# A GpSimd drain behind the last scatter of every span of 512 rows in the products stage

## The chip, the cores and the metric

The kernel runs on one core of one Trainium2 chip. The metric is the device time of one execution in microseconds (us); the median of three runs stands for the kernel.

## The reference

The program is a chain of three layers over 8 batches of 3072 tokens of 256 numbers:

```python
x = np.fft.fft(np.fft.fft(x, axis=1), axis=2).real       # transform
logits = x[:3072] @ w_gate                               # routing: one of 8 experts a token,
idx = argmax(logits); gate = softmax(logits)[idx]        # the first 768 tokens of each are kept
h = relu(disp @ w1[e]);  y = h @ w2[e]                   # experts, 256 -> 1024 -> 256
x = gate * y  (kept tokens; all other rows are 0)
a = x @ mw1;  b = x @ mw2                                # gated product layer
out = ((a * b) @ w3) @ w_out
```

(The routing runs over all 24576 tokens; since a row that is not kept gives zeros, the last layer is needed for the 8 x 768 = 6144 kept rows alone.)

## The kernel before, in words

The kernel has three stages. The transform stage computes the Fourier transforms of three batches (of the third, half the rows) on TensorE, routes their tokens, and scatters the kept rows into a table in DRAM (`disp`) with 61 indirect DMAs that GpSimd issues (L509). The experts' stage reads that table expert by expert and leaves its result transposed in SBUF (`yt`, 256 x 6144); meanwhile SyncE writes zeros over the whole output.

The third stage is `products` (L854 and after). It takes the 6144 rows in 12 spans of 512 (`spans`). For a span, `ysplit` makes a high part (ScalarE cast, L159) and a low part (a GpSimd subtraction, L160, tile `yl`) of each half of `yt`, two GpSimd instructions a span. `product` then runs eight times: the two matrix products with three TensorE passes each (L163 to L165), ScalarE copies one out of PSUM, VectorE multiplies by the other (L884), and the product is split again (L159 ScalarE, L160 VectorE). `project` multiplies the eight products of the span before by the fused matrix `Wc` (L896 to L898), 128 rows at a time; ScalarE scales each result by its gate (L900, tile `o`), and GpSimd scatters the 128 rows to their tokens' rows of the output with an indirect DMA (L901). So a span has four scatters, the stage 48. `project` of a span is called after the second `product` of the next one; that of the last span is called at the end. `ysplit` of span n+1 is written down after all of span n's products, but its tiles come from a pool of two buffers (`p_yc`), so it runs as soon as the products of span n-1 have let go of theirs.

The order on the engines in this stage is the scheduler's: the part of the program whose order is given by hand ends ahead of `mlp.products(main)` (L1063). Each engine takes its instructions in order. On GpSimd the stage's queue is: four scatters, two `yl`, four scatters, two `yl`, and so on. The scatters don't wait for one another (`declare_no_dep`); a scatter waits for its `o`.

Behind the stage every engine loads a flag (L1068) and branches (L1069) past a block that repeats the whole work over all batches; with these inputs the block is skipped. On the way past it GpSimd waits for the semaphores of its DMAs and raises them (INC_SWDGE_SEM, L1069). Then the program ends with drains and a barrier of all engines (L1151). GpSimd has a drain among these; the program's beginning has one too (L1144).

Of the kernel before, what the change touches and what calls it, by code (L numbers as in the profile page):

```python
# [125 lines left out]
def body(tc, cap, x, w_gate, w1, w2, mw1, mw2, w3t, w_out, cF, cS, cM, cR, cG, cI, cH, cT, out):  # L126
    nc = tc.nc
# [27 lines left out]
    def pool(name, bufs, stack, **k):  # L155
        return stack.enter_context(tc.tile_pool(name=name, bufs=bufs, reuse_waits="tile", **k))

    def split(hi, lo, src, eng=nc.vector):
        nc.scalar.copy(hi, src)  # L159
        eng.tensor_sub(lo, src, hi.bitcast(F32))  # L160

    def three(ps, wh, wl, ah, al, first, last):
        nc.tensor.matmul(ps, wh, ah, start=first, stop=False)  # L163
        nc.tensor.matmul(ps, wh, al, start=False, stop=False)  # L164
        nc.tensor.matmul(ps, wl, ah, start=False, stop=last)  # L165
# [384 lines left out]
    class Mlp:  # L550
# [303 lines left out]
        def products(self, stack):  # L854

            p_yc = pool("p_yc", 2, stack)
            p_g = pool("p_g", 10, stack)
            p_t = pool("p_t", 2, stack)
            pa = pool("pa", 2, stack, space=PSUM)
            pb = pool("pb", 2, stack, space=PSUM)  # L860
            po = pool("po", 3, stack, space=PSUM)
            yt, WM, Wc = self.yt, self.WM, self.Wc
            scat = []

            def ysplit(r0, n):
                ys = []
                for m in range(2):
                    hi = p_yc.tile([128, 512], F32R, name=f"yh{m}")[:, :n]
                    lo = p_yc.tile([128, 512], F32R, name=f"yl{m}")[:, :n]
                    split(hi, lo, yt[:, m, r0 : r0 + n], nc.gpsimd)  # L870
                    ys.append((hi, lo))
                return ys

            def product(ys, n, f):
                fs = slice(f * 128, f * 128 + 128)
                a = pa.tile([128, 512], F32, name="ps_a")[:, :n]
                b = pb.tile([128, 512], F32, name="ps_b")[:, :n]
                for w, ps in ((0, a), (1, b)):
                    for k in range(2):
                        three(ps, WM[w][0][:, k, fs], WM[w][1][:, k, fs], *ys[k], k == 0, k == 1)  # L880
                sa = p_t.tile([128, 512], F32, name="sa")[:, :n]
                nc.scalar.copy(sa, a)  # L882
                g = p_t.tile([128, 512], F32, name="g")[:, :n]
                nc.vector.tensor_mul(g, b, sa)  # L884
                hi = p_g.tile([128, 512], F32R, name="gh")[:, :n]
                lo = p_g.tile([128, 512], F32R, name="gl")[:, :n]
                split(hi, lo, g)
                return hi, lo

            def project(r0, n, gs):  # L890
                for t in range(n // 128):
                    col = r0 // 128 + t
                    ps = po.tile([128, 256], F32, name="ps_o")
                    ts = slice(t * 128, t * 128 + 128)
                    for f, (hi, lo) in enumerate(gs):
                        nc.tensor.matmul(ps, hi[:, ts], Wc[0][:, f], start=f == 0, stop=False)  # L896
                        nc.tensor.matmul(ps, hi[:, ts], Wc[1][:, f], start=False, stop=False)  # L897
                        nc.tensor.matmul(ps, lo[:, ts], Wc[0][:, f], start=False, stop=f == 7)  # L898
                    o = p_t.tile([128, 256], F32, name="o", bufs=3)
                    nc.scalar.activation(o, ps, AF.Copy, scale=gate2[:, col : col + 1])  # L900
                    i = nc.gpsimd.indirect_dma_start(  # L901
                        out=out[:, :],
                        out_offset=bass.IndirectOffsetOnAxis(ap=toki[:, col : col + 1], axis=0),
                        in_=o,
                        in_offset=None,
                        bounds_check=TOK - 1,
                        oob_is_err=False,
                    )
                    for q in scat:
                        tc.declare_no_dep(i.ins, q.ins, reason="every token has a row of its own")  # L910
                    scat.append(i)

            done = None
            spans = [(r, min(512, ROWS - r)) for r in range(0, ROWS, 512)]
            ys = ysplit(*spans[0])
            for n, (r0, w) in enumerate(spans):
                gs = []
                for f in range(8):
                    gs.append(product(ys, w, f))
                    if f == 1 and done:  # L920
                        project(*done)
                if n + 1 < len(spans):
                    ys = ysplit(*spans[n + 1])
                done = (r0, w, gs)
            project(*done)


# [227 lines left out]
```

## Time and profile before

| | us |
|---|---|
| median of three runs | 837.95 (837.57 to 837.99) |
| the profiled execution, its own time | 836.56 |
| its span, first to last instruction | 834.8 |
| TensorE busy in the span | 802.4 (96%) |
| GpSimd busy in the span | 149.6 (18%) |
| from the end of the last scatter's record to the end of the span | 14.7 |

The profile is of one execution. A busy time is that of the engine's data path; a drain, a branch, a semaphore instruction or a register load counts as none of it and appears only under its source line, on the engine's sequencer (POOLq is GpSimd's, SPq SyncE's). Of an indirect DMA the profile has two things: a record on GpSimd's own row, and the time from issue until its data has landed.

### The profile page before, as it was taken

The page shows a single profiled execution, that of the slowest core. Times are in us where ns is not written, and L with a number is a line of the kernel's source. Part 1 is how long each engine was busy: PE and PEld are TensorE (multiplying, and loading weights), DVE is VectorE, ACT ScalarE, POOL GpSimd, SP SyncE. Part 2 cuts the span into 40 slices and gives each one's busy share as a digit, 9 for nine tenths or more (in the row PEclk, how much of TensorE's full clock was granted, in tenths as well). Part 3 has the DMA queues.
Part 4 walks back from the last instruction along what each step waited for, and adds up shares of the span by engine and source line. Part 5 has one row for each costly group of instructions (what it writes and reads, how often), then busy time and mean ns, then how long its engine had stood idle before and what let it go on. Part 6 is the DMA issues. An engine that isn't in the chain of part 4 may idle for free.

```text
span 834.8 us, 12890 instructions
## 1 busy us (share of the span) xinstructions
PE 802.4 (96%) x5032; PEld 738.0 (88%) x5032; DVE 453.9 (54%) x874; ACT 370.0 (44%) x756; POOL 149.6 (18%) x139
## 2 busy tenths in 40 slices
PE   9999899799999999999999999999999999999992
PEld 8788799699999999999979899898898998988981
DVE  5676675498878787898542523424225234242230
ACT  2555665265545454565443433424334234243230
POOL 0047588000000000000023112121131122111101
PEclk9999899799999999999999999999999999999996
DMA  9945698476849474877100000000000000000000
GB/s 237 259 132 182 200 316 273 125 220 239 260 147 279 147 245 149 259 219 259 66 1 20 7 27 13 13 26 2 25 20 6 26 14 14 26 7 20 25 10 22
DMA packets 68822, 94.65 MB, mean 113 GB/s; under 512 B 5036, under 2 KB 56280, under 8 KB 67696
## 3 DMA queue, kind: packets, MB, share of 16 engines
q1 hardware_dynamic: 63552, 80.90, 32.0%
q0 software_dynamic: 5200, 12.84, 4.3%
q8 instruction: 41, 0.67, 0.3%
q14 instruction: 29, 0.24, 0.1%
HBM read 55.72 MB, written 39.63 MB: 114 GB/s over the span
## 4 chain that ended last, share of the span: by engine, by line
PE 80%; issue 9%; DVE 4%; DMA 3%; POOL 2%; ACT 1%; POOLq 0%; ACTq 0%; DVEq 0%; SPq 0%
PE ps_h L164 5%; PE ps_h L163 5%; PE ps_y L164 5%; PE ps_h L165 5%; PE ps_y L165 5%; PE ps_y L163 5%; PE ps_a L164 4%; PE ps_b L165 4%; PE ps_a L165 4%; PE ps_b L164 4%; PE ps_b L163 4%; PE ps_a L163 4%; PE ps_o L898 4%; PE ps_o L897 4%; PE ps_o L896 4%
## 5 line engine op out<-in xcount | busy, mean ns | idle before, releaser
L884 DVE TENSOR_TENSOR g<-ps_b,sa 128x512 f32<-128x512 f32 x96 | 66.2, 690 | 185.8 <-PE ps_b L165 179.2
L159 ACT CAST gh<-g 128x512 fp32r<-128x512 f32 x96 | 59.6, 620 | 132.9 <-DVE g L884 131.8
L160 DVE TENSOR_TENSOR gl<-g,gh 128x512 fp32r<-128x512 f32 x96 | 76.8, 800 | 65.9 <-ACT gh L159 65.9
L807 ACT ACTIVATE hh<-ps_h 128x256 fp32r<-128x256 f32 (+1 forms) x160 | 67.8, 427 | 97.3 <-PE ps_h L165 92.3
L897 PE MATMUL ps_o<-wcl,gh 128*128 128x256 f32 x384 | 108.7, 283 | 0.0
L898 PE MATMUL ps_o<-wch,gl 128*128 128x256 f32 x384 | 108.7, 283 | 0.0
L896 PE MATMUL ps_o<-wch,gh 128*128 128x256 f32 x384 | 108.6, 283 | 0.0
L160 POOL TENSOR_TENSOR yl<-yt,yh 128x512 fp32r<-128x512 f32 x24 | 30.5, 1288 | 419.5 <-ACT yh L159 419.5
L808 DVE SCALAR_TENSOR_TENSOR hl<-ps_h,hh 128x256 fp32r<-128x256 f32 (+1 forms) x160 | 74.8, 472 | 33.7 <-ACT hh L807 33.3
L509 POOL DMA_INDIRECT disp<-O,sloti x61 | 71.4, 1171 | 75.2 <-DVE acc L523 49.1
L901 POOL DMA_INDIRECT out_dram<-o,toki x48 | 47.0, 979 | 175.2 <-ACT o L900 175.2
L163 PE MATMUL ps_a<-yh,wm0h 128*128 128x512 f32 x192 | 75.0, 390 | 1.0 <-ACT yh L159 1.0
L164 PE MATMUL ps_a<-yl,wm0h 128*128 128x512 f32 x192 | 75.0, 391 | 0.7 <-POOL yl L160 0.7
L164 PE MATMUL ps_b<-yl,wm1h 128*128 128x512 f32 x192 | 74.7, 389 | 0.0
L165 PE MATMUL ps_a<-yh,wm0l 128*128 128x512 f32 x192 | 74.7, 389 | 0.0
L163 PE MATMUL ps_b<-yh,wm1h 128*128 128x512 f32 x192 | 74.7, 389 | 0.0
L165 PE MATMUL ps_b<-yh,wm1l 128*128 128x512 f32 x192 | 74.7, 389 | 0.0
L896 PEld LDWEIGHTS ps_o<-wch,gh 128*128 128x128 f32 x384 | 73.7, 192 | 0.5
L897 PEld LDWEIGHTS ps_o<-wcl,gh 128*128 128x128 f32 x384 | 73.7, 192 | 0.5
L898 PEld LDWEIGHTS ps_o<-wch,gl 128*128 128x128 f32 x384 | 73.7, 192 | 0.0
L900 ACT ACTIVATE o<-ps_o,gate 128x256 f32<-128x256 f32 x48 | 22.8, 475 | 104.7 <-PE ps_o L898 104.7
L882 ACT COPY sa<-ps_a 128x512 f32<-128x512 f32 x96 | 56.3, 587 | 11.6 <-PE ps_a L165 11.4
(179 smaller groups left out, 1952.9 us busy)
## 6 DMA issues: line engine op xcount, KB each, us to landing
out_dram<-zer SPq DMA_DIRECT2D x48, 512.0 KB, 6.5
raw<-in_w_dram SPq DMA_DIRECT2D x44, 512.0 KB, 5.2
xr<-in_x_dram SPq DMA_DIRECT2D x11, 768.0 KB, 8.4
raw<-in_w3t_dram SPq DMA_DIRECT2D x16, 512.0 KB, 4.8
raw<-in_mw_dram SPq DMA_DIRECT2D x8, 512.0 KB, 4.3
X<-disp SPq DMA_DIRECT2D x12, 266.0 KB, 4.2
X<-disp SPq DMA_DIRECT2D x8, 399.0 KB, 6.0
raw<-in_w_out_dram SPq DMA_DIRECT2D x4, 512.0 KB, 4.7
```

What stands on the lines that cost most here:

```text
L159: nc.scalar.copy(hi, src)
L160: eng.tensor_sub(lo, src, hi.bitcast(F32))
L163: nc.tensor.matmul(ps, wh, ah, start=first, stop=False)
L164: nc.tensor.matmul(ps, wh, al, start=False, stop=False)
L165: nc.tensor.matmul(ps, wl, ah, start=False, stop=last)
L509: i = nc.gpsimd.indirect_dma_start(out=disp[:, :], out_offset=bass.IndirectOffsetOnAxis(ap=sloti[0:w, g : g + 1], axis=0), in_=o[0:w, j, c ...
L807: nc.scalar.activation(hi, ps, AF.Relu)
L808: nc.vector.scalar_tensor_tensor(lo, ps, 0.0, hi.bitcast(F32), ALU.max, ALU.subtract)
L884: nc.vector.tensor_mul(g, b, sa)
L896: nc.tensor.matmul(ps, hi[:, ts], Wc[0][:, f], start=f == 0, stop=False)
L897: nc.tensor.matmul(ps, hi[:, ts], Wc[1][:, f], start=False, stop=False)
L898: nc.tensor.matmul(ps, lo[:, ts], Wc[0][:, f], start=False, stop=f == 7)
```

## The change

`project` issues one drain on GpSimd behind the last of its scatters. `i` is that scatter; `tc.issue_after(i.ins)` orders the drain behind it in GpSimd's queue and adds no wait of its own. Nothing else is changed.

```diff
                     for q in scat:
                         tc.declare_no_dep(i.ins, q.ins, reason="every token has a row of its own")
                     scat.append(i)
+                with tc.issue_after(i.ins):
+                    nc.gpsimd.drain()
 
             done = None
             spans = [(r, min(512, ROWS - r)) for r in range(0, ROWS, 512)]
```

There are 12 such drains in the executed path. `products` is called a second time inside the block that is skipped.

## Rows read from the trace of the kernel before

**Rows 1.** The page's busy times, and its 40 slices of the span.
```profile
PE 802.4 (96%) x5032; PEld 738.0 (88%) x5032; DVE 453.9 (54%) x874; ACT 370.0 (44%) x756; POOL 149.6 (18%) x139
PE   9999899799999999999999999999999999999992
POOL 0047588000000000000023112121131122111101
```

**Rows 2.** Busy time of each engine in stretches of the products stage and behind it.
```profile
core 0: us, PE busy (x) PEld busy (x) DVE busy (x) ACT busy (x) POOL busy (x), PEclk, DMA share, GB/s
480.00:520.00 40.00, 40.00 (x250) 36.24 (x249) 12.70 (x17) 14.22 (x25) 8.42 (x8) 1.00 0.05 18
640.00:680.00 40.00, 40.00 (x228) 35.27 (x227) 16.41 (x21) 16.05 (x29) 9.01 (x8) 1.00 0.04 14
825.00:834.00 9.00, 0.00 (x0) 0.00 (x0) 0.00 (x0) 0.00 (x0) 0.00 (x0) 0.50 0.00 0
```

**Rows 3.** GpSimd's timeline in the products stage: start, duration, instruction, idle before and releaser.
```profile
458.25 0.97 POOL L901 DMA_INDIRECT out_dram<-o,toki  x1 [1.95 <-ACT o L900]
473.88 2.54 POOL L160 TENSOR_TENSOR yl<-yt,yh 128x512 fp32r<-128x512 f32 x2 [14.65 <-ACT yh L159]
...
507.18 2.54 POOL L160 TENSOR_TENSOR yl<-yt,yh 128x512 fp32r<-128x512 f32 x2 [14.65 <-ACT yh L159]
...
782.56 0.97 POOL L901 DMA_INDIRECT out_dram<-o,toki  x1 [23.64 <-ACT o L900]
...
810.42 0.97 POOL L901 DMA_INDIRECT out_dram<-o,toki  x1 [18.20 <-ACT o L900]
...
819.10 0.97 POOL L901 DMA_INDIRECT out_dram<-o,toki  x1 [1.95 <-ACT o L900]
```

**Rows 4.** Waits in the products stage: who for whom, us in total, times, longest.
```profile
PEld ps_a L164 <- POOL yl L160: 1.6, 2, 0.8
PE ps_a L164 <- POOL yl L160: 0.7, 2, 0.4
```

**Rows 5.** The last pieces of the chain that ended last: start, duration, what.
```profile
817.15 1.72 issue
818.87 0.49 POOLq L1068
819.36 0.71 POOL out_dram L901
```

**Rows 6.** GpSimd's sequencer by line behind the stage: durations in ns (min/median/max), first and last start.
```profile
L1068 POOLq TENSOR_LOAD <-flagi x1: 492/492/492, 818.9 to 818.9; - x1
L1069 POOLq COMPARE_BRANCH  x1: 53/53/53, 819.4 to 819.4; - x1
L1069 POOLq EVENT_SEMAPHORE  x5: 17/43/43, 822.1 to 822.5; - x5
L1069 POOLq INC_SWDGE_SEM  x1: 2368/2368/2368, 822.6 to 822.6; - x1
L1151 POOLq DRAIN  x3: 40/107/8967, 825.0 to 834.5; - x3
```

**Rows 7.** The last line of Rows 6 cut to 824 to 834 us.
```profile
L1151 POOLq DRAIN  x1: 8967/8967/8967, 825.0 to 825.0; - x1
L1151 POOLq EVENT_SEMAPHORE  x1: 17/17/17, 834.0 to 834.0; - x1
```

**Rows 8.** The stage's scatters by line, and their way from issue to landing.
```profile
L901 POOL DMA_INDIRECT out_dram<-o,toki x48: 972/975/997, 449.6 to 819.1; - x48
DMA to landing us min/median/max: 2.4/2.4/2.5
```

**Rows 9.** DMA traffic from 822.8 us to 834.7 us.
```profile
DMA packets 0, 0.00 MB, mean 0 GB/s; under 512 B 0, under 2 KB 0, under 8 KB 0
```

**Rows 10.** The program's beginning on GpSimd's sequencer (L1144), and the transform stage's scatters.
```profile
L1144 POOLq INC_SWDGE_SEM  x1: 27/27/27, 0.1 to 0.1; - x1
L1144 POOLq DRAIN  x1: 189/189/189, 0.3 to 0.3; - x1
...
L509 POOL DMA_INDIRECT disp<-O,sloti x61: 914/977/2018, 50.4 to 147.0; - x61
```

## The prediction

> **What bounds the kernel now.** I read the page's 40 slices first: TensorE is at nine tenths or more in nearly every slice but the first and the last, GpSimd at one or two tenths in the products stage, and the last slice is almost empty for both [rows 1]. Then the stage's stretches: in the middle of it TensorE is busy 40.00 of 40 us, GpSimd some 8 to 9 [rows 2]. So within the stage nothing that GpSimd does costs time as long as TensorE finds its operands. That leaves the end. By the chain's last pieces, GpSimd's register load (818.87) and the last scatter (819.10, 0.97 us, so over at 820.07) come last [rows 3, 5], and after them no engine's data path does anything. The rest of the span, 834.8 - 820.07 = 14.7 us, is to be read on GpSimd's sequencer, by source line [rows 6, 7]: register load from 818.87, branch at 819.4, first instruction behind the branch at 822.1, INC_SWDGE_SEM 2.37 us from 822.6, and then one drain from 825.0 that lasts **8.967 us**, to 834.0. The final barrier is 0.8 us behind it. So this drain is the bound of the end of the program: whatever shortens it or moves it shows one for one.
>
> What does it wait for? Not for data: the last scatter lands 2.4 us after issue, at 821.5 [rows 8], and from 822.8 us on no DMA packet moves [rows 9]. Not for a matmul or a vector instruction: from 825 to 834 every engine is at zero [rows 2]. And a drain on GpSimd isn't long in itself: the other two of the program's end take 40 and 107 ns [rows 6], the one at the beginning 189 ns [rows 10]. The long one differs in what GpSimd did since the drain before it: 61 + 48 = 109 scatters [rows 8, 10], and the INC_SWDGE_SEM straight ahead of it. The trace doesn't tell which of these it pays for. That is the whole question of this change.
>
> **The change, part by part.** It adds 12 drains; it removes and moves nothing.
>
> *Eleven drains inside the stage.* Behind each stands, on GpSimd's queue, the two low parts `yl` or the next scatter. After the fourth scatter of a span (458.25 + 0.97 = 459.22) GpSimd has nothing to do until 473.88, 14.65 us [rows 3]; ten spans look like this, and the two gaps without `yl` are 23.64 and 18.20 us [rows 3]. The dearest drain that the trace shows is 8.97 us; it fits into the shortest of these gaps with 5.7 us to spare. If the cover were gone: `yl` is written one period ahead of its use, since it fills the second of two buffers. The period is 507.18 - 473.88 = 33.30 us, the two instructions take 2.54, so TensorE would feel a drain only if it held GpSimd up for some 14.65 + 30 = 45 us. TensorE waited for `yl` only at the start of the stage, 0.7 us in all (1.6 us on its weight loads) [rows 4], ahead of the first drain. Nothing else is queued behind a drain; ScalarE waits for scatters' landings to reuse `o`, and the drains stand behind the scatters. Cost of these eleven: **0**, by either price.
>
> *The twelfth drain, behind the last scatter.* Three things happen. First, GpSimd's sequencer now can't run ahead: before, it loaded the flag at 818.87, while the last scatter still ran; now it gets there only when the scatter is over, at 820.07. That is **+1.2 us** on everything behind it [rows 3, 5]. Second, the drain's own length d. Third, the long drain at 825.0 may get shorter.
>
> *The price of a drain.* Bounds by rows: from below 0.04 us, from above 8.97 us [rows 6]. Between them I read the long drain as work that GpSimd put off and that the drain makes it do: the drain behind it costs 107 ns with nothing left to do, so 8.967 - 0.107 = 8.86 us belongs to the backlog, and spread over 109 scatters that is an estimate of 81 ns for each. I take this reading because something other than a fixed wait must have been left over: GpSimd idled for 14 to 24 us at a time between scatters, all data had landed, and yet 9 us remained at the end. Then the first drain of the stage pays for 61 + 4 scatters, 65 x 81 ns = 5.3 us, and the other ten for 4 each, 0.33 us: all inside the gaps. The twelfth pays 0.33 + 0.107 = 0.4 us on the path. The long drain at the end falls to the nearest row with nothing outstanding, 0.107 us.
>
> Sum: +1.2 (the sequencer held) + 0.4 (twelfth drain) - 8.86 (the long drain) = **-7.3 us**. Against the profiled execution's own 836.56 us (span 834.8, so 1.8 us lie around it) that is 829.3; the median of the runs, 837.95, is 1.4 us above the profiled one, and the forecast is made on it: 837.95 - 7.3 = **830.7 us**.
>
> Its own range: INC_SWDGE_SEM, 2.37 us at the end but 0.03 at the beginning [rows 6, 10], might shrink with the backlog (-2.3, 828.3); of the scatter part, only some may be cleared early (to 831.5 if about 0.8 us stays). So 828.2 to 831.5 for this case.
>
> **The rivals.**
>
> *1. A drain only waits for GpSimd's own instructions, and the long one pays for INC_SWDGE_SEM.* Then the eleven drains and the twelfth cost 0.04 to 0.19 us each, the long one stays at 8.97, and only the held sequencer is left: +1.2 + 0.1 = +1.3, 839.3 us. For it: the long drain follows INC_SWDGE_SEM without a gap, and all scatters were long over. Against it: the program's beginning has an INC_SWDGE_SEM too, and the drain behind it took 0.19 us [rows 10], though that one may have had nothing to raise. The Trainium skill says in "PSUM — Partial Sum Buffer", section "Engine vs sequencer instructions", that a drain waits for the engine to go fully idle. By that rule alone nothing could be put off to a drain from scatters whose records ended long before, and the sum would be this rival's; the trace neither contradicts nor confirms it, since what GpSimd does in these 9 us has no record.
>
> *2. A fixed charge once a scatter has been issued.* The first drain behind any scatter costs 8.97 us, however many there were, and the next one without scatters in between 0.1. The eleven are hidden all the same. The twelfth costs 8.97 on the path, the last falls to 0.107: +1.2 + 8.97 - 8.86 = +1.3, 839.3 us, the same as rival 1 by another way. If the drain also waits for the landing (821.5 instead of 820.07) it is 1.4 more, 840.7. For it: short drains follow the long one at once. Against it: nothing in the trace, since no drain stands behind a few scatters alone.
>
> *3. The charge is paid twice: slower.* As rival 2, but INC_SWDGE_SEM behind the twelfth drain brings the charge back, so that the long drain stays: +1.2 + 8.97 = +10.2, 848.1 us. The place is the twelfth drain alone. It decides from the point where twelfth drain and rest together exceed what the long one gives back; with the long one at 0.107 that is at d = 8.86 - 1.2 = 7.7 us. For it: a scatter and an INC_SWDGE_SEM both stand ahead of the long drain, and each may carry its part. Against it: it needs two causes of about the same size where one explains the row.
>
> *4. The order.* The scheduler gives this stage's order; 12 more instructions could shift it. It would have to put a scatter or `yl` over 30 us later to be felt, so I give it little, and nearly all of that to small losses.
>
> **How the numbers follow.** The backlog read off the trace (830.7): 0.50. Rival 1 (839.3): 0.18. Rival 2: 0.15, of it 0.11 at 839.3 and 0.04 with the landing, 840.7. Rival 3 (848.1): 0.14. Order and the like, slower: 0.03. About 0.2%, 1.7 us, is what a measurement of this kernel can tell from no change; so 836.3 to 839.6 counts as the same. Faster: 0.50. Same: 0.18 + 0.11 = 0.29. Slower: 0.04 + 0.14 + 0.03 = 0.21. The range reaches from the first case's lower end over rivals 1 and 2, 828.2 to 841.0, and leaves out rival 3 and most of the order, under 0.2 together. The likeliest case's own range is 828.2 to 831.5.
>
> **What would show it.** In the changed kernel, GpSimd's drains by line: eleven in the gaps behind the fourth scatters, the first of them longest (5 us by the backlog; all alike, 9 us, by rivals 2 and 3; all near 0.1 by rival 1), the twelfth from 820.1 us, and the length of the drain behind INC_SWDGE_SEM: 0.1 us by the backlog and rival 2, 9 us by rivals 1 and 3. The register load should start not before the twelfth drain's end. TensorE should be busy 40 of 40 us in the stage as before, with its last matmul at the same time, and `yl` should start at the same times in the period. What would make the prediction wrong: a twelfth drain of more than 2 us, or a last drain that stays above 1 us; and in the stage, any wait of TensorE for `yl`.

## The result

The changed kernel takes 830.95 us (median of six runs, 827.18 to 833.75) against 837.97 us (837.44 to 839.72) for the kernel before: 7.0 us less, a ratio of 0.9909 with a 95% interval of 0.9887 to 0.9930. The forecast was 830.7, in a range of 828.2 to 841.0. A second measurement (the run e7 below) gave 830.70 against 837.84, ratio 0.9906 (0.9885 to 0.9926). Every ratio here compares, of each kernel, the runs within 1.5% of its own fastest: on the slower chip of e1 and e2 these are six of the seventeen runs of the kernel before, all six of e1 and nine of e2's twelve.

GpSimd's sequencer in the changed kernel, by source line, durations in ns (min/median/max), then first and last start in us. L913 is the new drain; L1070, L1071 and L1153 are the lines that were L1068, L1069 and L1151 [rows 6, 7].

```profile
L913 POOLq DRAIN  x12: 2850/2857/6588, 454.7 to 815.5; - x12
L1070 POOLq TENSOR_LOAD <-flagi x1: 499/499/499, 820.1 to 820.1; - x1
L1071 POOLq INC_SWDGE_SEM  x1: 189/189/189, 823.6 to 823.6; - x1
L1153 POOLq DRAIN  x3: 46/53/107, 823.9 to 825.1; - x3
L1153 SPq DRAIN  x3: 7/7/13, 824.5 to 824.8; - x3
```

The reader is to see three things. The drain of the program's end is now 0.05 us, after 8.97. INC_SWDGE_SEM, which the change doesn't touch, is 0.19 us after 2.37. And the register load starts at 820.1, long after the last scatter:

```profile
454.89 0.97 POOL L901 DMA_INDIRECT out_dram<-o,toki  x1 [1.96 <-ACT o L900]
470.52 2.54 POOL L160 TENSOR_TENSOR yl<-yt,yh 128x512 fp32r<-128x512 f32 x2 [14.66 <-ACT yh L159]
...
815.75 0.97 POOL L901 DMA_INDIRECT out_dram<-o,toki  x1 [1.95 <-ACT o L900]
```

This is GpSimd's timeline (start, duration, instruction, idle before). The idle time ahead of `yl` is 14.66 us, as before [rows 3]: the drain in that gap cost the queue nothing. From the last scatter's end (816.72) to the end of the span (825.4) it is 8.7 us, where it was 14.7: the tail lost **6.0 us**.

The two spans differ by more, 834.8 - 825.4 = 9.4 us. The other 3.35 us lie ahead of all drains: the last scatter starts at 815.75 instead of 819.10, the stage's others are as much earlier, and the difference arises in the transform and experts' stages. There one and the same ScalarE instruction starts at 137.8 us before and at 141.2 in the changed kernel, a later one at 160.9 and 157.4, so the changed kernel is first behind and then ahead. Here the stretch from 150 to 200 us (busy time of each engine, then the granted clock), the changed kernel first, with a stretch of the products stage below it:

```profile
150.00:200.00 50.00, 49.01 (x345) 48.21 (x346) 41.30 (x87) 26.94 (x57) 0.00 (x0) 1.00 0.71 228
480.00:520.00 40.00, 40.00 (x250) 36.24 (x249) 12.02 (x16) 13.60 (x24) 8.91 (x9) 1.00 0.06 21
```

```profile
150.00:200.00 50.00, 47.82 (x324) 46.88 (x325) 38.89 (x82) 24.74 (x53) 0.00 (x0) 0.92 0.69 222
```

From 150 to 200 us the granted clock was 1.00 in the changed kernel's profile and 0.92 on average in the other. No instruction of that stretch is changed, so I count this as the difference between two executions, not as the change's. The profiled execution of the changed kernel is also its fastest (827.18). Within the products stage TensorE is busy 40.00 of 40 us, as before [rows 2].

### The profile page after: what moved, and what is told of

It is laid out like the page before. It is cut to its first block, busy times and chain, and to the rows that moved or that the text cites. A ratio compares the mean times of both kernels' runs of the same rounds, so it can differ in the third digit from the quotient of the medians.

```text
span 825.4 us, 12902 instructions
## 1 busy us (share of the span) xinstructions
PE 803.3 (97%) x5032; PEld 738.3 (89%) x5032; DVE 453.9 (55%) x874; ACT 369.6 (45%) x756; POOL 147.6 (18%) x139
## 4 chain that ended last, share of the span: by engine, by line
PE 79%; issue 9%; DVE 4%; POOL 2%; DMA 2%; ACT 1%; POOLq 1%; DVEq 0%; ACTq 0%; SPq 0%
PE ps_y L164 5%; PE ps_h L164 4%; PE ps_a L164 4%; PE ps_h L165 4%; PE ps_h L163 4%; PE ps_b L165 4%; PE ps_a L165 4%; PE ps_b L164 4%; PE ps_y L165 4%; PE ps_b L163 4%; PE ps_a L163 4%; PE ps_y L163 4%; PE ps_o L898 4%; PE ps_o L897 4%; PE ps_o L896 4%
## 5 line engine op out<-in xcount | busy, mean ns | idle before, releaser
L509 POOL DMA_INDIRECT disp<-O,sloti x61 | 69.4, 1138 | 75.5 <-DVE acc L523 49.6
```

The costliest lines, as they stand in the source:

```text
L509: i = nc.gpsimd.indirect_dma_start(out=disp[:, :], out_offset=bass.IndirectOffsetOnAxis(ap=sloti[0:w, g : g + 1], axis=0), in_=o[0:w, j, c ...
```

## The experiments

The theory after this result: every scatter leaves something behind, which the next drain works off at a fixed price each; besides, a drain lasts at least until the scatters ahead of it have landed. Rivals: a fixed charge that some drain has to pay once; a charge of the last drain alone.

**e1, only the twelfth drain.**

```diff
-                with tc.issue_after(i.ins):
-                    nc.gpsimd.drain()
+                if r0 // 512 == 11:
+                    with tc.issue_after(i.ins):
+                        nc.gpsimd.drain()
```

> Only the drain behind the last span's scatters is kept; the eleven inside the stage are gone. Backlog theory: this one drain has all 109 scatters to work off and does on the path what the drain of the program's end did before: it runs on for 8 to 11 us behind the last scatter's record, INC_SWDGE_SEM and the end's drain are short (0.2 and 0.1 us), and the time is that of the kernel before plus what the held sequencer costs, 0 to +3 us, so 838 to 841. Rival, a fixed charge that a drain ahead of the branch and INC_SWDGE_SEM avoids: the one drain lasts as long as the twelfth did (3.3 us behind the scatter's record) and the time is that of the changed kernel, about 831.

Measured, GpSimd's sequencer by line:

```profile
L914 POOLq DRAIN  x1: 10180/10180/10180, 870.1 to 870.1; - x1
L1072 POOLq INC_SWDGE_SEM  x1: 189/189/189, 883.9 to 883.9; - x1
L1154 POOLq DRAIN  x3: 34/41/107, 884.2 to 885.4; - x3
...
870.38 0.97 POOL L901 DMA_INDIRECT out_dram<-o,toki  x1 [1.95 <-ACT o L900]
```

The one drain runs on for 9.0 us behind the last scatter (which ended at 871.35; the drain at 880.3), and from that scatter to the end of the span it is 14.35 us, against 14.7 in the kernel before. The fixed charge that the last drain would buy off is out: without the eleven drains inside the stage nothing is won. The chip of this run was slower for every kernel, so only comparisons with the kernel before on that chip count (885.78 us there): 886.72 us, ratio 1.0103 (1.0029 to 1.0176). The medians of all runs lie 0.9 us apart and the tails 0.35 us the other way; the ratio's interval lies above 1 because it sets all six runs of e1 against the six fastest of seventeen, so it shows no loss.

**e2 and e8, eleven drains, the twelfth left out** (the condition is `r0 // 512 < 11`). The kernel ran twice, the second time beside the changed kernel.

> The eleven drains inside the stage are kept, the twelfth, behind the last span, is gone. Backlog theory: only four scatters are left over at the end; INC_SWDGE_SEM and the end's drain take 0.2 to 1 us together, and since GpSimd's sequencer may again load the flag and branch while the last scatter runs, the time is 3 to 4.5 us under that of the changed kernel: 826.5 to 828. Rival, a fixed charge for any scatter since the last drain, paid once: the end's drain is again near 9 us, and the time is that of the kernel before, 838. Rival, the twelfth drain is needed to keep INC_SWDGE_SEM short: INC_SWDGE_SEM takes 2.4 us again and the time is about 829.

> Eleven drains, none behind the last span, beside the changed kernel on the same chip. Backlog theory, now with the prices read from the runs: INC_SWDGE_SEM 0.27 us, the end's drain 0.37 us, and 4.4 us from the last scatter's end to the span's end, against 7 to 8.7 in the changed kernel: 2.5 to 4.3 us faster than the changed kernel, 9 to 11 us faster than the kernel before.

Measured in e2, then in e8:

```profile
L1072 POOLq INC_SWDGE_SEM  x1: 268/268/268, 877.9 to 877.9; - x1
L1154 POOLq DRAIN  x3: 46/107/371, 878.2 to 879.4; - x3
```

```profile
L1071 POOLq TENSOR_LOAD <-flagi x1: 500/500/500, 820.2 to 820.2; - x1
L1072 POOLq INC_SWDGE_SEM  x1: 268/268/268, 823.9 to 823.9; - x1
L1154 POOLq DRAIN  x3: 46/107/371, 824.2 to 825.5; - x3
...
820.47 0.97 POOL L901 DMA_INDIRECT out_dram<-o,toki  x1 [1.95 <-ACT o L900]
```

INC_SWDGE_SEM 0.27 and the drain 0.37 us, for four scatters, the same on both chips; the register load is ahead of the last scatter again (820.2 against 820.47), and from that scatter's end (821.44) to the end of the span (825.8) it is 4.4 us. e2's time is unclear on its chip: 875.37 us against 885.78 by the medians of all runs, 0.988, but a ratio of 0.9964 (0.9908 to 1.0021) by the runs that a ratio compares. e8 took **827.45 us** against 837.84, ratio 0.9875 (0.9851 to 0.9900): 3.25 us below the changed kernel on the same chip (e7, 830.70), as expected. Its median is the lowest of this study. "A fixed charge for any scatter since the last drain" is out: four scatters cost 0.4 us, not 9.

**e7, the changed kernel again.**

> The changed kernel once more, beside the next one on the same chip. Backlog theory: twelfth drain ends 0.2 us behind the landing of the last scatter (2.4 to 4.1 us after its issue), INC_SWDGE_SEM 0.19 us, the end's drain 0.05 us; 14.7 us from the last scatter's end to the span's end become 7 to 8.7 us, and the time is 6 to 8 us below that of the kernel before.

```profile
L913 POOLq DRAIN  x12: 2842/2851/6587, 459.0 to 819.8; - x12
L1071 POOLq INC_SWDGE_SEM  x1: 189/189/189, 827.8 to 827.8; - x1
L1153 POOLq DRAIN  x3: 46/53/107, 828.1 to 829.3; - x3
```

The time is 830.70 us, 7.1 below the kernel before; from the last scatter's end (821.03) to the end of the span (829.6) 8.6 us, as in the first profile. The durations agree to some 20 ns, but for the twelfth drain: 4.39 us here, 4.50 there.

**e3, only the first drain** (the condition is `r0 // 512 == 0`).

> Only the drain behind the first span's scatters is kept (65 scatters ahead of it). Backlog theory, 60 to 115 ns a scatter: that drain again runs 5.4 us behind the scatter's record, and the 44 scatters of the other eleven spans are left for the end: INC_SWDGE_SEM and the end's drain together 3 to 6 us instead of 11.3. A fixed charge would leave them at 11.3 us together, or at 2 to 3 us as for four scatters.

```profile
L914 POOLq DRAIN  x1: 6588/6588/6588, 506.2 to 506.2; - x1
L1072 POOLq INC_SWDGE_SEM  x1: 1068/1068/1068, 870.7 to 870.7; - x1
L1154 POOLq DRAIN  x3: 46/107/3647, 871.8 to 876.0; - x3
```

44 scatters were left, and the end pays 1.07 + 3.65 = 4.7 us, in the forecast's span of 3 to 6. (One run: 878.07 us, on e1's chip.)

**e4, drains far behind the landings, at unequal distances.**

```diff
-        eng.tensor_sub(lo, src, hi.bitcast(F32))
+        return eng.tensor_sub(lo, src, hi.bitcast(F32))
...
-                    split(hi, lo, yt[:, m, r0 : r0 + n], nc.gpsimd)
+                    i = split(hi, lo, yt[:, m, r0 : r0 + n], nc.gpsimd)
                     ys.append((hi, lo))
+                if r0 // 512 in (1, 3, 4, 6, 10):
+                    with tc.issue_after(i.ins):
+                        nc.gpsimd.drain()
```

> No drain stands behind scatters. Five drains stand behind the GpSimd subtractions of the spans with the indices 1, 3, 4, 6 and 10, so that all data of the scatters ahead of each has long landed, and 61, 4, 4, 8 and 16 scatters stand between one drain and the next; 16 are left for the end. Backlog theory: behind the subtraction's record the five last 3.7 to 5 us, twice 0.2 to 0.5, 0.4 to 0.9 and 0.8 to 1.9 us, in proportion to the count, and INC_SWDGE_SEM with the end's drain 0.9 to 2 us. If a drain only waits for landings, all five end with the subtraction (under 0.2 us behind it).

The drains of four stretches (the first holds the one behind 61 scatters, the second the two behind 4, then 8, then 16), and the subtractions that they stand behind:

```profile
L874 POOLq DRAIN  x1: 8580/8580/8580, 465.1 to 465.1; - x1
L874 POOLq DRAIN  x2: 2299/2304/2309, 521.0 to 554.3; - x2
L874 POOLq DRAIN  x1: 2629/2629/2629, 620.9 to 620.9; - x1
L874 POOLq DRAIN  x1: 3279/3279/3279, 754.1 to 754.1; - x1
```

```profile
463.63 5.02 POOL L160 TENSOR_TENSOR yl<-yt,yh 128x512 fp32r<-128x512 f32 x4 [295.55 <-ACT yh L159]
520.33 2.54 POOL L160 TENSOR_TENSOR yl<-yt,yh 128x512 fp32r<-128x512 f32 x2 [14.66 <-ACT yh L159]
...
620.23 2.54 POOL L160 TENSOR_TENSOR yl<-yt,yh 128x512 fp32r<-128x512 f32 x2 [14.65 <-ACT yh L159]
...
753.43 2.54 POOL L160 TENSOR_TENSOR yl<-yt,yh 128x512 fp32r<-128x512 f32 x2 [14.65 <-ACT yh L159]
```

A drain's record begins while the subtraction still runs, so what counts is its end less the subtraction's: for 61 scatters 465.1 + 8.58 - 468.65 = 5.0 us; for 4, 521.0 + 2.31 - 522.87 = 0.4; for 8, 620.9 + 2.63 - 622.77 = 0.76 (0.72 by the unrounded start); for 16, 754.1 + 3.28 - 755.97 = 1.4. At the end, for another 16:

```profile
L1072 POOLq INC_SWDGE_SEM  x1: 508/508/508, 869.1 to 869.1; - x1
L1154 POOLq DRAIN  x3: 46/107/1351, 869.7 to 871.6; - x3
```

The price doesn't depend on how long ago the scatters landed: the 61 had ended 300 us before, and nobody had paid for them in between. (One run: 873.63 us, on e1's chip.) With these runs the end's two terms make a table:

| scatters since the drain before | INC_SWDGE_SEM, ns | drain, ns | kernel |
|---|---|---|---|
| 0 | 189 | 41, 53 | e1, changed |
| 4 | 268 | 371 | e2, e8 |
| 16 | 508 | 1351 | e4 |
| 44 | 1068 | 3647 | e3 |
| 109 | 2368 | 8967 | before |

From the first row and the last: (8967 - 41) / 109 = **82 ns** a scatter for the drain, (2368 - 189) / 109 = **20 ns** for INC_SWDGE_SEM. By these two the rows between should be 369, 1353, 3649 and 269, 509, 1069: all are met within 3 ns. The GpSimd subtractions between the drains (none for the four scatters, 18 for the 44) don't count. Nor does the time since the drain before: the first drain of the stage, with 65 scatters, takes 6.588 us when it comes at 454.7 us (changed kernel) and when it comes at 506.2 us (e3).

**e5, fewer rows to a scatter.**

```diff
-                        out_offset=bass.IndirectOffsetOnAxis(ap=toki[:, col : col + 1], axis=0),
-                        in_=o,
+                        out_offset=bass.IndirectOffsetOnAxis(ap=toki[0:16, col : col + 1], axis=0),
+                        in_=o[0:16],
```

> The kernel before, with each of the 48 output scatters cut from 128 rows to the first 16 (the other rows of the output are left out); no drain is added. The end's drain took 41 ns + 82 ns a scatter in the runs so far, and INC_SWDGE_SEM 189 ns + 20 ns a scatter. If the backlog counts scatters, both stay as in the kernel before, 8.97 and 2.37 us. If it counts rows or descriptors, only an eighth of the 48 is left, as from 61 + 6 scatters: 5.5 us and 1.5 us.

```profile
L1069 POOLq INC_SWDGE_SEM  x1: 2368/2368/2368, 823.1 to 823.1; - x1
L1151 POOLq DRAIN  x3: 40/107/8975, 825.5 to 835.1; - x3
```

Unchanged: the backlog counts instructions, not rows. The time, 837.15 us, is the kernel before's.

**e6, 48 plain DMAs more on GpSimd.**

```diff
                     scat.append(i)
+                    nc.gpsimd.dma_start(out=spare[col * 128 : col * 128 + 128], in_=o[:, 0:8])
```

> The kernel before, with 48 plain DMAs added on GpSimd's queue, one of 128 x 8 numbers into a spare DRAM tile behind each output scatter; no drain is added. If the backlog counts every DMA that GpSimd issues, the end's drain takes 157 x 82 ns = 12.9 us and INC_SWDGE_SEM 3.3 us. If it counts indirect DMAs alone, 8.97 and 2.37 us as before.

```profile
L1071 POOLq INC_SWDGE_SEM  x1: 1195/1195/1195, 824.4 to 824.4; - x1
L1153 POOLq DRAIN  x3: 40/107/4157, 825.7 to 830.4; - x3
...
656.11 0.99 POOL L902 DMA_INDIRECT out_dram<-o,toki  x1 [1.32 <-ACT o L901]
658.73 0.58 POOL L913 DMA_DIRECT2D spare<-o  x1 [1.64 <-issue]
```

Neither answer: 4157 ns and 1195 ns are those of (4157 - 41) / 82 = 50 scatters, with 157 DMAs issued. With no drain added and 48 DMAs more the kernel was faster than before in its one run, 832.84 against 837.84 us. In GpSimd's timeline one thing stands out: a single plain DMA, the 115th DMA that GpSimd issues, starts 1.64 us late, with nothing that the profile shows it to wait for. Two more runs went into this.

**e9, 24 plain DMAs more** (`if col % 2:` ahead of the same line), and **e10, 48 scatters more** (128 rows of 8 numbers each, to a spare tile).

> The kernel before with 24 plain DMAs more on GpSimd's queue (behind every second scatter), so 133 DMAs of GpSimd in all; no drain is added. With 48 more (157 in all) the 115th started 1.6 us late and the end's drain took 4.16 us, as from 50. If something cleared the backlog once, at about the 115th, leaving 7 behind, 133 leave 26 here: end's drain 2.2 us, INC_SWDGE_SEM 0.7 us, and again one late start at the 115th. If plain DMAs themselves don't count and 50 was 48 scatters with two more, or if the backlog is held at 50 from some point on, the end's drain is near 4.1 us again.

> The kernel before with 48 more scatters on GpSimd's queue, each of 128 rows of 8 numbers into a spare DRAM tile, 157 indirect DMAs in all; no drain is added. If what cleared the backlog is the number of GpSimd's DMAs, of whatever kind, the 115th starts late again and the end's drain takes 4.2 us as with 48 plain DMAs. If it was the plain DMAs' own doing, nothing starts late and the end's drain takes 157 x 82 ns = 12.9 us.

e9, then e10:

```profile
L1072 POOLq INC_SWDGE_SEM  x1: 715/715/715, 824.7 to 824.7; - x1
L1154 POOLq DRAIN  x3: 44/107/2197, 825.5 to 828.2; - x3
...
728.20 0.58 POOL L914 DMA_DIRECT2D spare<-o  x1 [1.66 <-issue]
```

```profile
L1082 POOLq INC_SWDGE_SEM  x1: 1191/1191/1191, 825.6 to 825.6; - x1
L1164 POOLq DRAIN  x3: 40/107/4148, 826.8 to 831.5; - x3
...
656.71 0.97 POOL L903 DMA_INDIRECT out_dram<-o,toki  x1 [0.63 <-ACT o L902]
659.83 0.98 POOL L914 DMA_INDIRECT spare<-o,toki  x1 [2.14 <-issue]
```

e9's drain is that of (2197 - 41) / 82 = 26 DMAs, the 133 - 107 that was forecast; e10's is that of 50. The late start is there in both, at the 115th DMA again: 1.66 us in e9, where a plain DMA otherwise follows its scatter at once, and 2.14 us in e10, where the added scatter otherwise starts 0.30 us behind the one before. So plain and indirect DMAs count alike, and at the 115th GpSimd itself gets rid of some 107 of them, for 1.6 to 1.8 us, much less than the 8.8 us that a drain takes for as many. The kernel before, with 109, ended just short of that. (One run each: e9 830.31 us, e10 833.59, the kernel before 837.49 beside them.) In e6 and e10 the 115th starts after the 114th has landed (2.46 and 2.44 us after its issue, so at 658.57 and 659.15 us); whether it waits for that, why it is the 115th, and why it is cheaper there, the runs don't show.

## Why the prediction was right, and where its terms were off

*The stage.* Right as written: TensorE busy throughout, `yl` with the same idle time ahead of it, and the eleven drains hidden. The first was put at 5.3 us; it ends 454.7 + 6.59 - 455.86 = 5.4 us behind its scatter. One reading was off without harm: nine spans, not ten, have the gap of 14.65 us, which with the two longer gaps makes the eleven.

*The price of a drain.* Right: a backlog of 81 ns a scatter was the estimate, 82 ns the measurement, in proportion over 4 to 109 scatters. Rival 1 falls with e1: there the drain that runs on for 9.0 us has no INC_SWDGE_SEM ahead of it, and the one behind INC_SWDGE_SEM takes 41 ns. Rivals 2 and 3, a fixed charge, fall with e8, rival 3 also with the changed kernel itself (0.05 us). Rival 4: the waits are those of before.

*The twelfth drain was mis-sized.* It was put at 0.4 us behind the scatter; it is 3.3 us, and so beyond the 2 us that the prediction itself had named as a sign of being wrong: the register load was to start at 820.07 - 818.87 = 1.2 and 0.4 later, and starts 820.06 - 816.72 = 3.3 us behind the scatter's end where it had started 1.2 us ahead of it, +4.5 instead of +1.6 us. What I had named under rival 2 and left out of the likeliest case is true: a drain doesn't end before its scatters have landed. The landing time of the last scatter, and of the fourth of the span before, from issue, in the changed kernel:

```profile
DMA to landing us min/median/max: 4.1/4.1/4.1
...
DMA to landing us min/median/max: 2.4/2.4/2.4
```

The drains behind these two (the second group is of the drains 2 to 11), and the earlier one's scatter:

```profile
L913 POOLq DRAIN  x1: 4497/4497/4497, 815.5 to 815.5; - x1
...
L913 POOLq DRAIN  x10: 2850/2856/2862, 488.0 to 787.7; - x10
...
787.89 0.97 POOL L901 DMA_INDIRECT out_dram<-o,toki  x1 [1.95 <-ACT o L900]
```

The last landed at 815.75 + 4.1 = 819.85 and its drain ended at 815.5 + 4.50 = 820.0; in the other the drain, too, ends 0.2 us behind the landing (2.86 us from 0.23 ahead of the issue), some 1.65 us behind its scatter's record instead of the 0.33 that was forecast for it. In e7 the last scatter took 4.0 us and the drain ended as close behind it. Where the backlog takes longer than the landing, as in e1 and the first drain, the landing is hidden in it; where the data has landed, as in e4, four scatters cost 0.4 us.

So 1.65 of the 3.3 us belong to a landing of the usual 2.4 us, and the other 1.64 to the last scatter's late one. The drain didn't make it late: in e8 the last scatter but one, with no drain behind it, landed 4.4 us after its issue, and in e5, which adds no drain, the last two took 3.4 and 4.2 us, where the stage's usual time is 2.0. In the kernel before, the landings of the last two scatters aren't in the trace, so the 2.4 us of [rows 8] are of others. What goes with a late landing is a DMA packet of 16 KB on a queue that the profile calls `instruction`. In e7, which has all 48 landings, seven took 3.2 to 4.0 us and the rest 2.4 to 2.5; while the packets of each of the seven move, such a packet runs too, and it does for none of the rest. In the changed kernel one runs from 817.4 to 818.6 us. Of the last scatter's 48 packets 45 start by then, and 3 only behind it:

```profile
q0 software_dynamic: 45, 0.12, 25.3%
q8 instruction: 1, 0.02, 5.5%
...
q0 software_dynamic: 3, 0.01, 3.6%
```

These are DMA queues (q0 carries the scatter) with packets, MB and share of time, from 817.2 to 818.6 and from 818.6 to 819.9 us. That the instruction packet holds up the three is my reading; no run takes it away.

On what a drain waits for the Trainium skill and the runs part. The Trainium skill's rule in "PSUM — Partial Sum Buffer", section "Engine vs sequencer instructions", that a drain waits for the engine to go fully idle, is too narrow here: GpSimd's drain waited for landings and for a backlog of DMAs whose records had long ended (e4: 5.0 us for scatters 300 us old).

*INC_SWDGE_SEM was mis-sized the other way.* It stood in the sum with no change and in the range with -2.3; it fell by 2.18 us, at 20 ns a scatter.

*What comes late next.* Not in the prediction: with GpSimd's drain over at 823.9, SyncE's own last drain (824.5 to 824.6) is now what the barrier waits for, 0.65 us of the long drain's gain.

The tail's sum as measured: +4.5 (register load) - 0.1 (branch and semaphores) - 2.2 (INC_SWDGE_SEM) - 8.9 (long drain) + 0.65 (SyncE) = **-6.0 us**, where -7.3 was forecast. The medians say -7.0, with an interval of some 5.9 to 9.5 us; the forecast's closeness to them, 830.95 against 830.7, is partly luck: two terms were off by +2.9 and -2.2 us, the tail gave 1.3 us less than forecast, and the remaining 1.0 us of the medians' difference isn't traced to the change. The runs of the changed kernel spread over 6.6 us, those before over 2.3; what spreads them isn't settled.

## What to carry to other kernels

On GpSimd, look at the drain of the program's end: if it is long, divide it by the DMAs that GpSimd issued since the drain before (here that holds up to 109 DMAs; past 114 the count had fallen back). A drain in an idle stretch of GpSimd took that time off the end here; one behind the last DMA doesn't pay, since it waits for its landing and holds up the sequencer's way out (e8 against e7). The sum of a tail has to name what is late next on every engine (here SyncE, 0.65 us) and what else pays by the same count (here INC_SWDGE_SEM).

## What the runs showed of the hardware

- A drain on GpSimd takes 82 ns for each DMA, plain or indirect, that GpSimd issued since its last drain, whatever its rows (16 or 128) and its age (up to 300 us), and 41 ns besides, over 0 to 109 DMAs; INC_SWDGE_SEM takes 20 ns for each, and 189 ns.
- It lasts at least until the DMAs ahead of it have landed, and some 0.2 us more (2.4 us landing: 2.85 us drain; 4.1 us landing: 4.50 us).
- GpSimd started the 115th DMA since the last drain 1.6 to 1.8 us late (e6, e9, e10), and at the end some 107 fewer were left to pay for (26 of 133, 50 of 157).
- Seven of the 48 scatters of e7 landed 3.2 to 4.0 us after issue, the others 2.4 to 2.5; the seven are those whose packets met one of 16 KB on an `instruction` queue, with a drain behind them or not. What sends that packet is open.
